# Transposing an MLP mixer's input by DMA instead of on TensorE, from the third batch on

## The chip, the cores and the metric

The kernel runs on one core of a Trainium2 chip. The metric is the device time of one execution in microseconds; lower is better. Most executions of one kernel here lie within about 0.7% of its median, a few 0.8 to 1.1% above it, so verdicts rest on several interleaved runs of both kernels on the same chip.

## The reference, cut to what matters

Eight batches, eight heads, 576 positions, 64 channels a head. First an attention with a causal mask and a decay, then an MLP mixer over tokens and channels:

```python
def _moe_ref(x, w_tok1, w_tok2, w_ch1, w_ch2):       # x: 8 x 576 x 512, from the attention
    xt = x.transpose(0, 2, 1)
    h = np.maximum(xt @ w_tok1, 0.0) @ w_tok2        # mixing over tokens
    u = x + h.transpose(0, 2, 1)
    h2 = np.maximum(u @ w_ch1, 0.0) @ w_ch2          # first and last layer over channels
    return (u + h2).astype(np.float32)
```

## The kernel before

As this kernel is written, each matmul sums over the partitions of its two operands (the first dimension of a tile). The mixing over tokens produces u with tokens on partitions, and the first channel layer wants channels there. So u is transposed once for each batch, in pieces of 128 tokens by 512 channels: each takes four 128x128 transposes on TensorE into one PSUM bank and one copy out of it.

The program is not written in order of execution. Every step is an operation with a modelled cost, given to a small list scheduler ("the planner"). The planner simulates the engines with these costs, gives out ring buffers, and writes each engine's instructions down in the order of its modelled start times. Each engine then executes its own list in order, as the traces show it (in the changed kernel ScalarE stands idle for 2.58 us at a square whose load is late, and four exponentials listed behind it start only after it). The costs are guesses, so a wrong one does not change the result, only the order.

```python
# in tok(b): one piece c of batch b; u, us: token-major, uT: channel-major
P.op(dve(512, add), reads=[(pm, 0)] + xkeys, writes=[ukey], prio=0)         # u = mixed + x, VectorE
if not odd and c == 4:
    continue
pt = Buf(r_mx, False)                                                       # one of three PSUM banks
# ...
def tr(pt=pt, dst=dst, di=di):
    o = pt.t[:, :].bitcast(BF16)
    for m in range(NMC):                                                    # NMC = 4
        nc.tensor.transpose(out=o[:, m * 128 : m * 128 + 128],
                            in_=dst.t[:, di, m * 128 : m * 128 + 128], identity=ident[:, :])
P.op({"PE": (4 * 0.057, 4 * 0.057 + 0.3, tr)}, reads=rk, writes=[(pt, 0)] + ..., prio=(rank - TOK, 2))
# ... then a copy to uT by ScalarE or VectorE
P.op(either(512, lambda ev=ev: ev(0), lambda ev=ev: ev(1), True), reads=[(pt, 0)], writes=[(uT, c)], prio=0)
```

The last 64 tokens of two neighbouring batches share one piece (`us`), so even batches have four pieces and odd ones five. In chan(b) the first layer reads uT with 48 (or 2 x 48) matmuls, and the last layer follows. The scheduler runs the last layer of batch b-1 into the mixing of batch b.

Of the kernel before, what the change touches and what calls it, by code (L numbers as in the profile page):

```python
# [204 lines left out]
def c_pe(n, f32=False):  # L205
    occ = n * (4 if f32 else 1) / 2400.0 + 0.0025
    return occ, occ + 0.30
# [126 lines left out]
def kernel(  # L334
# [12 lines left out]
    nc = tc.nc  # L347
# [25 lines left out]
    def ring(name, n, shape, dt, pool=None):  # L373
        p = pool or fast
        return Ring(name, [p.tile(shape, dt, name=f"{name}{i}", tag=f"{name}{i}") for i in range(n)])
# [39 lines left out]
    r_mx = ring("pmx", 3, [128, 512], FP32, psum)  # L415

    P = Plan()
# [29 lines left out]
    for i in range(1, 3):  # L447
        P.op({"DVE": (1.0, 1.2, lambda i=i: pads(nc.vector, i)), "POOL": (1.6, 1.8, lambda i=i: pads(nc.gpsimd, i))},
             writes=[("pad", i)], prio=40)
    P.op({"DVE": (0.6, 0.8, lambda: pads2(nc.vector)), "POOL": (1.0, 1.2, lambda: pads2(nc.gpsimd))},  # L450
         writes=["padw"], prio=41)
    P.op({"DVE": (0.3, 0.5, lambda: pads3(nc.vector, 1)), "POOL": (0.5, 0.7, lambda: pads3(nc.gpsimd, 1))},
         writes=["padv"], prio=42)
# [12 lines left out]
    def dve(n, fn, two=False):  # L466
        return {"DVE": (*c_dve(n, two), fn)}

    def act(n, fn, bias=False):
# [4 lines left out]
         reads=["s"], writes=["sr"], prio=-1)  # L474
    P.op({"DVE": (1.3, 1.6, lambda: nc.vector.tensor_tensor_scan(
        out=cum[:, :], data0=one_sb[:, :], data1=s_sb[:, :], initial=0.0, op0=ALU.mult, op1=ALU.add))},
        reads=["sr"], writes=["cum"], prio=-1)
    P.op(dve(1, lambda: nc.vector.tensor_scalar(
        out=half[:, :], in0=cum[:, S - 1 : S], scalar1=-0.5, scalar2=None, op0=ALU.mult)),
        reads=["cum"], writes=["half"], prio=-1)  # L480
    P.op(act(576, lambda: nc.scalar.activation(
        out=wn[:, 0:S], in_=cum[:, :], func=AF.Exp, bias=half[:, 0:1], scale=1.0), True),
        reads=["half", "cum"], writes=["wn"], prio=-1)
    bw = Buf(r_mx, False)

    def w_tr():
# [6 lines left out]
        out=wT[:, :, :].rearrange("p c e -> p (c e)"), in_=bw.t[:, 0:384])),  # L493
        reads=[(bw, 0)], writes=["wT"], prio=-1)
# [18 lines left out]
        out=pre[:, :], data0=one_sb[:, :], data1=wn[:, 0:S], initial=0.0, op0=ALU.mult, op1=ALU.add))},  # L513
        reads=["wn"], writes=["pre"], prio=50)
# [255 lines left out]
    def either(n, fa, fd, two=False):  # L770
        return {"ACT": (*c_act(n), fa), "DVE": (*c_dve(n, two), fd)}

    def tok(b):
        odd = b % 2
        x = xbuf[b]
        h1 = Buf(r_h1)
        xkeys = [(x, hh) for hh in range(H)]
        rank = 4 * (b + 1) + LAG
        if odd:
            u = Buf(r_ub)  # L780
        else:
            u = Buf(r_ua)
            ushare[b // 2] = Buf(r_us)
        us = ushare[b // 2]
        heads = [(0, H - 2), (H - 2, H)] if b == 0 else [(0, H)]
        pms = [Buf(r_mx, False) for t in range(NTC)]
        for (ha, hb) in heads:
            for t in range(NTC):
                def mm(t=t, pm=pms[t], ha=ha, hb=hb):
                    for c in range(NJ):  # L790
                        nc.tensor.matmul(out=pm.t[:, ha * D : hb * D],  # L791
                                         lhsT=w1[:, NJ if odd and c == NJ - 1 else c, t * 128 : t * 128 + 128],
                                         rhs=x.t[:, c, ha * D : hb * D], start=(c == 0), stop=(c == NJ - 1))
                occ = 5 * c_pe((hb - ha) * D)[0]
                P.op({"PE": (occ, occ + 0.3, mm)},
                     reads=[(x, hh) for hh in range(ha, hb)] + ["w1", "w1s", "padw"],
                     writes=[(pms[t], ha)], holds=[h1], prio=(rank - TOK, 0))
        for t in range(NTC):
            pm = pms[t]
            P.op(either(512,  # L800
                        lambda t=t, pm=pm: nc.scalar.activation(out=h1.t[:, t, :], in_=pm.t[:, :], func=AF.Relu),
                        lambda t=t, pm=pm: nc.vector.tensor_scalar_max(out=h1.t[:, t, :], in0=pm.t[:, :], scalar1=0.0)),
                 reads=[(pm, ha) for (ha, hb) in heads], writes=[(h1, t)], prio=0)
        uT = Buf(r_uTb if odd else r_uTa)
        for c in range(NJ):
            dst, di, lo, hi = (u, c, 0, 128) if c < NJ - 1 else (us, 0, 64 * odd, 64 * odd + 64)
            pm = Buf(r_mx, False)

            def mm(c=c, pm=pm):
                w0 = c * 128 + (64 if c == NJ - 1 and not odd else 0)  # L810
                for t in range(NTC):
                    nc.tensor.matmul(out=pm.t[:, :], lhsT=w2[:, t, w0 : w0 + 128],
                                     rhs=h1.t[:, t, :], start=(t == 0), stop=(t == NTC - 1))
            P.op({"PE": (2 * c_pe(512)[0], 2 * c_pe(512)[0] + 0.3, mm)}, reads=[(h1, 0), (h1, 1), "w2"],
                 writes=[(pm, 0)], holds=[dst], prio=(rank - TOK, 1))
            ukey = (dst, di, lo)

            def add(c=c, pm=pm, dst=dst, di=di, lo=lo, hi=hi):
                nc.vector.tensor_tensor(out=dst.t[lo:hi, di, :], in0=pm.t[lo:hi, :], in1=x.t[lo:hi, c, :], op=ALU.add)  # L819
            P.op(dve(512, add), reads=[(pm, 0)] + xkeys, writes=[ukey], prio=0)  # L820

            if not odd and c == 4:
                continue
            pt = Buf(r_mx, False)
            rk = [(us, 0, 0), (us, 0, 64)] if dst is us else [ukey]
            tc_ = c

            def tr(pt=pt, dst=dst, di=di):
                o = pt.t[:, :].bitcast(BF16)
                for m in range(NMC):  # L830
                    nc.tensor.transpose(out=o[:, m * 128 : m * 128 + 128], in_=dst.t[:, di, m * 128 : m * 128 + 128],
                                        identity=ident[:, :])
            P.op({"PE": (4 * 0.057, 4 * 0.057 + 0.3, tr)}, reads=rk, writes=[(pt, 0)] + ([("st", "uT")] if b == 1 else []), holds=[uT], prio=(rank - TOK, 2))

            def ev(eng, pt=pt, tc_=tc_):
                i = pt.t[:, :].bitcast(BF16)[:, 0:512].rearrange("p (m t) -> p m t", m=NMC)
                o = uT.t[:, :, tc_ * 128 : tc_ * 128 + 128]
                if eng == 0:
                    nc.scalar.copy(out=o, in_=i)  # L839
                else:  # L840
                    nc.vector.tensor_copy(out=o, in_=i)
            P.op(either(512, lambda ev=ev: ev(0), lambda ev=ev: ev(1), True), reads=[(pt, 0)], writes=[(uT, c)], prio=0)
        return u, us, uT
# [75 lines left out]
    for b in range(B):  # L919
        for h in range(0, H, 2):  # L920
            pair(b, h)
        st = tok(b)
        chan(b, *st)

    P.op(dve(64, lambda: nc.vector.tensor_scalar(
        out=bad[0:PR, 4:], in0=sq[:, :], scalar1=21.0, scalar2=None, op0=ALU.is_gt)),
        reads=[("sq", i) for i in range(NSQ)] + ["bad0"], writes=["bad"], prio=50)
# [3 lines left out]
         reads=["bad"], writes=[(bf, 0)], prio=(100, 0))  # L931
# [17 lines left out]
    for o in [o for o in order if o.eng == "PE"]:  # L949
# [3 lines left out]
        while t1 - t0 > 0.06:  # L953
# [6 lines left out]
            if not slots:  # L960
# [4 lines left out]
                out=t[:, 0:n], lhsT=zero[:, 0:128], rhs=zero[:, 0:n], start=True, stop=True)  # L965
# [47 lines left out]
```

## Time and profile before

| | before |
|---|---|
| median of three runs | 339.69 us (338.54 to 340.94) |
| profiled execution, span | 337.3 us |
| TensorE busy / share of the last chain | 93% / 69% |
| transposes of u on TensorE | 144, of which 108 for b = 2 to 7 |
| output store of 256 KB on the sync queue, medians | issue 0.33 to 0.36 us, landing (data arrived) from 2.0 us after the start of issue |

The main lines stand in the prediction. In TensorE's timeline, columns are start, duration, engine, source line, operation, output and inputs, shapes, count. In b = 3 of the kernel before:

```profile
148.05 0.39 PE L831 MATMUL pmx_117<-ident,us_103 128*128 128x128 bf16 x4
148.49 0.38 PE L657 MATMUL psc_112<-qT_80,kT_83 128*128 128x512 bf16 x1
```

A group of four transposes that is followed at once by work that is ready costs 0.22 us. This one holds TensorE for 0.44 us to the start of the next instruction, though the profile reports no idle time there: short gaps stay below what it lists. Nine of the 27 groups of b = 2 to 7 take 0.38 to 0.51 us in this way.

### The profile page before, as it was taken

Reading aid. Unit: us, or ns where it says so; the run is one execution under the profiler, and the core shown is the slowest. Engines: PE = TensorE matmul, PEld = TensorE weight load, DVE = VectorE, ACT = ScalarE, POOL = GpSimd, SP = SyncE. Lnnn points to the kernel's source line nnn. Section 1 sums busy time; section 2 is a strip of 40 time slices with the busy share of each in tenths; the row PEclk is TensorE's granted clock in tenths of the full one; section 3 lists DMA queues with packets and bytes.
Section 4 is the critical chain, followed back from the end, with each engine's and each line's share of the span. In section 5 each row is a group of like instructions: output and inputs, shape, how many; then the busy total and the mean of one; then the engine's idle time right before and its main releaser. Section 6 shows DMA issues by size and latency. Waiting matters only on the chain.

```text
span 337.3 us, 6710 instructions
## 1 busy us (share of the span) xinstructions
PE 315.2 (93%) x2532; PEld 184.7 (55%) x2565; DVE 207.7 (62%) x510; ACT 221.6 (66%) x395; POOL 100.1 (30%) x137
## 2 busy tenths in 40 slices
PE   6978999988999999989999999989999999999992
PEld 2445585645765455555765445555765454446641
DVE  7698945899776746584577655584677545450021
ACT  4766975669788548785786747787799738325600
POOL 6355157768237001830147001830110000000000
PEclk9799999999999999999999999999999999999999
DMA  7999999999953349288024952253548110011031
GB/s 203 222 291 376 374 213 231 266 271 227 215 114 106 130 138 206 77 208 194 2 75 133 227 145 71 87 157 121 143 119 232 67 63 2 16 49 62 3 95 68
DMA packets 62584, 50.60 MB, mean 150 GB/s; under 512 B 39632, under 2 KB 55568, under 8 KB 62544
## 3 DMA queue, kind: packets, MB, share of 16 engines
q1 hardware_dynamic: 62544, 50.10, 56.7%
q8 instruction: 22, 0.36, 0.4%
q14 instruction: 18, 0.15, 0.2%
HBM read 40.65 MB, written 9.44 MB: 148 GB/s over the span
## 4 chain that ended last, share of the span: by engine, by line
PE 69%; DVE 18%; ACT 7%; issue 2%; DMA 1%; POOL 1%; SPq 0%; ACTq 0%
PE pmx_118 L877 9%; PE pmx_119 L877 8%; PE pmx_117 L859 8%; PE pmx_118 L859 8%; PE pmx_119 L859 8%; PE pmx_117 L877 7%; DVE ub_101 L819 3%; PE pmx_119 L791 2%; DVE E_86 L671 2%; PE psc_114 L657 2%; PE pav_115 L689 2%; PE psc_113 L657 2%; DVE E_84 L671 2%; PE pav_116 L689 2%; PE psc_112 L657 2%
## 5 line engine op out<-in xcount | busy, mean ns | idle before, releaser
L859 PEld LDWEIGHTS <-wc_70 128*128 128x128 bf16 x624 | 59.3, 98 | 30.5 <-issue 0.2
L877 PEld LDWEIGHTS <-gb_107 128*128 128x128 bf16 x240 | 22.9, 98 | 25.3
L575 POOL CAST qkn_76<-qkf_73 96x768 bf16<-96x768 f32 x22 | 19.1, 887 | 37.5 <-ACT gb_107 L866 20.1
L877 PEld LDWEIGHTS <-ga_106 128*128 128x128 bf16 x192 | 18.2, 98 | 21.2 <-issue 1.4
L575 POOL CAST qkn_77<-qkf_74 96x768 bf16<-96x768 f32 x19 | 15.7, 840 | 40.8 <-ACT ga_106 L866 19.7
L575 POOL CAST qkn_75<-qkf_72 96x768 bf16<-96x768 f32 x19 | 15.4, 828 | 39.1 <-ACT gb_107 L866 18.5
L671 DVE TENSOR_TENSOR E_84<-E_84,keep 128x256 bf16<-128x256 bf16 (+1 forms) x55 | 18.4, 365 | 13.3 <-ACT E_84 L663 12.8
L859 PE MATMUL pmx_118<-uTb_105,wc_70 128*128 128x320 bf16 x128 | 22.6, 299 | 0.1
L859 PE MATMUL pmx_117<-uTb_105,wc_70 128*128 128x320 bf16 x128 | 22.6, 299 | 0.0
L859 PE MATMUL pmx_119<-uTb_105,wc_70 128*128 128x320 bf16 x128 | 22.6, 299 | 0.0
L877 PE MATMUL pmx_119<-wc_71,gb_107 128*128 128x512 bf16 x92 | 22.3, 379 | 0.2
L548 POOL TENSOR_TENSOR vp_90<-vf_88,wT 128x512 bf16<-128x512 f32 (+1 forms) x20 | 21.0, 1069 | 2.5 <-DMA vf_88<-in_v_dram 2.2
L671 DVE TENSOR_TENSOR E_86<-E_86,keep 128x256 bf16<-128x256 bf16 (+1 forms) x50 | 17.1, 368 | 6.7 <-ACT E_86 L663 6.4
L671 DVE TENSOR_TENSOR E_85<-E_85,keep 128x256 bf16<-128x256 bf16 (+1 forms) x55 | 16.5, 329 | 6.3 <-ACT E_85 L663 6.1
L877 PE MATMUL pmx_118<-wc_71,gb_107 128*128 128x512 bf16 x80 | 19.2, 379 | 0.2
L866 ACT ACTIVATE gb_107<-pmx_119 128x320 bf16<-128x320 f32 x25 | 11.1, 444 | 11.4 <-PE pmx_119 L859 9.9
L859 PE MATMUL pmx_118<-uTa_104,wc_70 128*128 128x512 bf16 (+1 forms) x77 | 17.0, 335 | 0.2
L859 PE MATMUL pmx_119<-uTa_104,wc_70 128*128 128x512 bf16 (+1 forms) x79 | 17.1, 336 | 0.1
L548 POOL TENSOR_TENSOR vp_89<-vf_87,wT 128x512 bf16<-128x512 f32 (+1 forms) x15 | 15.3, 1040 | 5.8 <-PE pav_116 L689 4.7
L859 PE MATMUL pmx_117<-uTa_104,wc_70 128*128 128x512 bf16 (+1 forms) x78 | 16.8, 335 | 0.1
L877 PE MATMUL pmx_117<-wc_71,ga_106 128*128 128x512 bf16 x69 | 16.7, 379 | 0.2
L877 PE MATMUL pmx_118<-wc_71,ga_106 128*128 128x512 bf16 x69 | 16.5, 379 | 0.3 <-ACT uTb_105 L839 0.2
(297 smaller groups left out, 723.0 us busy)
## 6 DMA issues: line engine op xcount, KB each, us to landing
qkf_74<-in_k_dram SPq DMA_DIRECT2D x15, 288.0 KB, 3.4
qkf_74<-in_q_dram SPq DMA_DIRECT2D x15, 288.0 KB, 4.0
vf_87<-in_v_dram SPq DMA_DIRECT2D x16, 256.0 KB, 7.0
vf_88<-in_v_dram SPq DMA_DIRECT2D x16, 256.0 KB, 5.5
qkf_72<-in_k_dram SPq DMA_DIRECT2D x13, 288.0 KB, 4.0
qkf_72<-in_q_dram SPq DMA_DIRECT2D x13, 288.0 KB, 4.5
qkf_73<-in_k_dram SPq DMA_DIRECT2D x12, 288.0 KB, 4.7
qkf_73<-in_q_dram SPq DMA_DIRECT2D x12, 288.0 KB, 5.0
```

Of the source, the lines that this page charges most:

```text
L548: eng.tensor_tensor(out=vp.t[p0 : p0 + n, c, :, 0:D], in0=vf.t[p0 : p0 + n, c, :, :], in1=wT[p0 : p0 + n, cw, b * H : b * H + H].unsqueeze ...
L575: nc.gpsimd.tensor_copy(out=o, in_=a)
L657: nc.tensor.matmul(out=o[:, :, c0 : c0 + e - a], lhsT=kT.t[:, j0 : j0 + 128], rhs=qT.t[:, :, a:e], start=True, stop=True)
L671: nc.vector.tensor_tensor(out=E.t[:, :, d0 : d0 + n], in0=E.t[:, :, d0 : d0 + n], in1=keep[:, k0 : k0 + n].unsqueeze(1).to_broadcast([128, ...
L689: nc.tensor.matmul(out=o[:, ic, 0 : D + 1], lhsT=E.t[:, hh, d0 : d0 + 128], rhs=vp.t[:, jc, h + hh, 0 : D + 1], start=(jc == j_lo), stop=( ...
L791: nc.tensor.matmul(out=pm.t[:, ha * D : hb * D], lhsT=w1[:, NJ if odd and c == NJ - 1 else c, t * 128 : t * 128 + 128], rhs=x.t[:, c, ha * ...
L819: nc.vector.tensor_tensor(out=dst.t[lo:hi, di, :], in0=pm.t[lo:hi, :], in1=x.t[lo:hi, c, :], op=ALU.add)
L859: nc.tensor.matmul(out=pm.t[:, 0 : e - a], lhsT=wc1[:, m, cc * 128 : cc * 128 + 128], rhs=uT.t[:, m, a:e], start=(m == 0), stop=(m == NMC ...
L866: lambda cc=cc, pm=pm, a=a, e=e: nc.scalar.activation(out=g.t[:, cc, a:e], in_=pm.t[:, 0 : e - a], func=AF.Relu),
L877: nc.tensor.matmul(out=pm.t[:, :], lhsT=g.t[:, cc, c * 128 : c * 128 + 128], rhs=wc2[:, cc, :], start=(cc == 0), stop=(cc == NCC - 1))
```

## The change

The intent: TensorE is the bound (busy 93% of the span), the DMA engines have room after the second batch (mean share 1.06 from 40 to 80 us, 0.19 to 0.68 in the six transposing stretches of b = 2 to 7), so let a transposing DMA carry u to uT directly, without PSUM and without the copy.

```diff
-            pt = Buf(r_mx, False)
             rk = [(us, 0, 0), (us, 0, 64)] if dst is us else [ukey]
             tc_ = c
+            if b >= 2:
+                def trd(dst=dst, di=di, tc_=tc_):
+                    nc.sync.dma_start_transpose(out=uT.t[:, :, tc_ * 128 : tc_ * 128 + 128], in_=dst.t[:, di, :])
+                P.op({"SP": (0.6, 0, trd)}, reads=rk, writes=[(uT, c)],
+                     prio=0, dma=0.5)
+                continue
+            pt = Buf(r_mx, False)
```

The pair (0.6, 0) is what the planner is told: 0.6 us of the sync queue for each; `dma=0.5` is the time planned on the DMA engines.

## The prediction

> **What bounds the kernel now.** I read the page's busy shares first, then the chain of waits, then who waits on TensorE, then the six stretches in which batches 3 to 8 (b = 2 to 7) form the mixer's input, and last the timeline of the final one.
>
> ```profile
> span 337.3 us, 6710 instructions
> PE 315.2 (93%) x2532; PEld 184.7 (55%) x2565; DVE 207.7 (62%) x510; ACT 221.6 (66%) x395; POOL 100.1 (30%) x137
> PE 69%; DVE 18%; ACT 7%; issue 2%; DMA 1%; POOL 1%; SPq 0%; ACTq 0%
> ...
> 96.00:112.00 16.00, 15.38 (x142) 9.23 (x142) 12.33 (x29) 11.64 (x21) 9.37 (x12) 1.00 0.38 103
> ...
> L831 PE MATMUL pmx_118<-ident,ua_100 x24: 216/219/221, 39.1 to 261.2; 128*128 128x128 bf16 x24
> ...
> L839 ACT COPY uTb_105<-pmx_118 x5: 577/586/586, 145.4 to 299.3; 128x512 bf16<-128x512 bf16 x5
> ...
> L841 DVE COPY uTa_104<-pmx_118 x4: 407/414/425, 39.8 to 261.6; 128x512 bf16<-128x512 bf16 x4
> ```
>
> TensorE is busy 93% of the span and carries 69% of the chain that ends last. From 96 us on it is almost solid: 15.38 of the first 16 us, and likewise later. So the kernel is bound by the quantity of work on TensorE, and nearly every microsecond taken off it there ends the kernel earlier, as long as nothing new makes it wait. VectorE and ScalarE are not the bound in sum (62%, 66%), but in the transposing stretches they are: the table of those six stretches (columns: length, busy PE, PEld, DVE, ACT, POOL, clock, DMA share, GB/s) shows it.
>
> ```profile
> 102.70:111.00 8.30, 7.95 (x79) 4.88 (x79) 6.98 (x13) 6.06 (x12) 5.05 (x6) 1.00 0.42 112
> 141.40:150.00 8.60, 7.47 (x77) 4.64 (x77) 8.21 (x18) 6.71 (x12) 4.97 (x8) 1.00 0.55 164
> 179.70:187.30 7.60, 7.25 (x76) 4.57 (x75) 7.06 (x13) 4.78 (x9) 4.29 (x7) 1.00 0.46 120
> 217.00:226.00 9.00, 7.87 (x80) 4.81 (x80) 8.52 (x19) 7.05 (x14) 5.05 (x8) 1.00 0.56 160
> 255.60:263.30 7.70, 7.05 (x70) 4.28 (x70) 6.67 (x18) 7.61 (x14) 0.00 (x0) 1.00 0.68 184
> 293.80:305.10 11.30, 10.79 (x64) 5.40 (x63) 5.20 (x9) 2.15 (x4) 0.00 (x0) 1.00 0.19 71
> ...
> 146.69 0.38 PE L831 MATMUL pmx_119<-ident,ub_101 128*128 128x128 bf16 x4 [0.85 <-DVE us_103 L819]
> ...
> 222.37 0.38 PE L831 MATMUL pmx_119<-ident,ub_101 128*128 128x128 bf16 x4 [0.85 <-DVE us_102 L819]
> ```
>
> In two of them VectorE is busy 8.21 of 8.60 and 8.52 of 9.00 us, and TensorE stands 0.85 us at a transpose that waits for VectorE's addition. TensorE's idle time in the six sums to 52.50 - 48.38 = 4.1 us.
>
> [...] The trace shows TensorE's at 219 ns each, pipelined: a group of four that starts at 146.69 is followed by the next at 146.91, so four cost 0.22 us of TensorE[...]. No run yet shows the DMA's. [...] The landing I take from the trace: the output stores from the sync queue take 2.0 us at the median from issue to landing. [...]
>
> **The change part by part.** Odd b has five pieces of 128x512, even b four. For b = 2 to 7 that is 3 x 4 + 3 x 5 = 27 pieces.
> Removed from TensorE: 27 groups of four transposes, 27 x 0.225 = 6.1 us. TensorE is the path there, so all of it counts.
> Removed from ScalarE and VectorE: 27 evictions out of PSUM at 586 ns (ScalarE) or about 410 ns (VectorE), some 13 us. Little of this is on the path, but it comes out of exactly the six crowded stretches, and so do the rounds through the three PSUM banks that the transposes shared with the mixer's matmuls.
> Moved: in the built program's order the matmuls around those stretches keep their order, but the pieces of the previous batch's last layer (twelve matmuls, 2.6 us) now follow the mixer's matmuls at once, where TensorE used to meet transposes that had to wait for VectorE. The two waits of 0.85 us and smaller ones of 0.41, 0.30, 0.29, 0.16 and 0.16 us (the last two for an eviction) should mostly go; I count 2.3 of the 4.1 us of idle time.
> Added: 27 transposes on the sync queue, which issues a store in 0.33 to 0.36 us and waits most of the time. I take 1.2 us of that queue each [...] and 2.2 us from the end of issue to landing. Their 128 KB are 3.4 MB on top of 50.6 MB, and the DMA share in those stretches is 0.19 to 0.68.
> Is it hidden? Cover is the time from the first addition's end to the first matmul that needs the result. For even b = 4: the first addition ends at 181.5; after the last mixer matmul (182.8) the new order has 48 matmuls of 0.216 us of the last layer, 36 small ones of the attention (1.1 us), 7 score matmuls (1.5) and 12 small transposes (0.5), 13.5 us, so the result is needed at 196.3. Four serial transposes with 2 us of landing may cost 3.2 us each before anything waits. For odd b = 3: additions from 142.97 on, last mixer matmul done at 144.5, cover 36 x 0.216 + 1.1 + 1.1 + 0.3 = 10.2 us, needed at 154.7 to 155.2: five may cost 2.05 us each. For the last batch there is only the last layer to hide behind: 24 matmuls, 5.2 us, after 297.8; the left half is needed at 303.0, the right (pieces four and five) at 303.5. Additions end at 295.2, 295.8, 296.9, 297.5 and 299.0. With 1.2 us each, issue goes 295.2, 296.4, 297.6, 298.8, then a store, then the fifth from 300.4 to 301.6, landing at 303.8: 0.3 us too late.
> Sum: -6.1 - 2.3 + 0.3 = -8.1 us. From 339.7 that gives 331.6 us.
>
> **The rivals.** First: the transposes are slow, and a DMA wait takes the place of the evictions. [...] At 2 us each only the last batch stalls, by about 3.5 us: 335 us, inside 2%. At 3 us: about 5 us in each of b = 3 and 5 and 8.5 us at the end, less 8.4: some 350 us. [...]
> Second: the sync queue runs in order, so the transposes wait for additions and hold up the loads behind them, and they land behind loads already queued (q and k pieces land in 3.4 to 5.0 us, v in 5.5 to 7.0). For it: in the new order the transposes of b = 2 stand ahead of two stores and the next loads, and the page's DMA row reaches 8 and 9 tenths in places. Against it: three raw and three converted buffers of q and k let loads run several head pairs ahead, and GpSimd is only 30% busy; a load 5 us later should not reach TensorE. A queue of 5 us ahead of a transpose fits under the 10 and 13 us of cover, and the last batch has no loads about it. I put 1 us on it at most.
> Third: the transposing work is hidden anyway, so only the idle time changes. Against it: TensorE itself executes them, and its order is fixed.
> Fourth: it goes better. All 4.1 us of idle time vanish, and the lighter ScalarE and VectorE shorten waits elsewhere: 339.7 - 6.1 - 4.1 - 1 = 328.5 us.
>
> **Range and chances.** The steps add up to 331.6; a little for queueing makes it 332.0. The low end, 328.5, is the fourth rival; the high end, 340, is a transpose of about 2.4 us in both the odd stretches and the end. The line for faster by over 2% is 339.7 x 0.98 = 332.9, hardly above my number, so the chance of faster is 0.54 only; within 2% gets 0.32 (a transpose of 1.5 to 2.5 us), slower 0.14 (3 us and up, or something that I do not see).
>
> **What would show it.** Right: 108 fewer transposes and 27 fewer evictions; TensorE's busy time lower by about 6 us; the waits of 0.85 us gone from the odd stretches; no wait of the first-layer matmuls for a DMA into the transposed input beyond 1 us, except near the end of the last batch; transposes landing 2 to 4 us after issue, 1.2 us apart. Wrong: TensorE at the first layer waiting several us for a DMA in each batch (first rival); waits for converted q and k or for v (second); or busy time down by 6 us with as much new idle time.

## More of the kernel before

The kernel checks a range of q and k by squaring them on ScalarE. For the first two batches this is done late, from a second load:

```python
def stage_sq(b, h):                        # b = 0, 1 only; planned with low priority, lands in b = 5, 6
    for i, src in enumerate((k, q)):
        load_op(load, [(f, i)], ...)       # on the sync queue
    P.op({"ACT": (1.55, 2.0, lambda: nc.scalar.activation(out=junk[:, :], in_=f..., func=AF.Square, ...))}, ...)
```

## The result, and the profile after

The changed kernel takes 330.63 us (median of four runs, 328.07 to 333.03), before 339.88. The ratio is 0.9704, interval 0.9629 to 0.9779: faster by 3%. Ratios here are the mean time of one kernel's runs over that of the other's of the same rounds, so not quite the ratio of the medians. Executions over 1.5% slower than the fastest of the same kernel are left out of the means.

The head of the page of the changed kernel, against the same lines of before in the prediction:

```profile
span 330.5 us, 6536 instructions
PE 308.9 (93%) x2424; PEld 178.6 (54%) x2457; DVE 207.2 (63%) x511; ACT 207.4 (63%) x367; POOL 101.1 (31%) x137
PE 75%; DVE 14%; ACT 3%; DMA 3%; issue 2%; SPq 1%; POOL 0%; ACTq 0%
```

TensorE has 108 instructions fewer and 6.3 us less of busy time, ScalarE 28 fewer and 14 us less. VectorE has none fewer, although it lost 11 of the 27 evictions: the planner gave it 12 other evictions that ScalarE had made. The chain that ends last runs more through TensorE, and 3% of it through DMAs, where there was 1%. Of these 9.8 us, 5.76 are the first load at the start (4.55 before); the other 4.03 are new, and we come to them. First the transposes, by their source line (minimum/median/maximum in ns), and from the start of issue to landing:

```profile
L828 SPq DMA_TRANSPOSE uTa_104<-ua_100 x12: 1194/1218/1339, 107.9 to 255.3; - x12
L828 SPq DMA_TRANSPOSE uTb_105<-ub_101 x12: 1194/1216/1232, 143.4 to 294.3; - x12
...
DMA to landing us min/median/max: 2.4/2.4/4.2
```

At the median each holds the sync queue for 1.22 us (the one not shown, in b = 5, for 2.39) and has landed 2.4 us after its start. The place with the least cover is the last batch. In the changed kernel's timeline there:

```profile
290.37 5.14 SPq L828 DMA_TRANSPOSE uTb_105<-ub_101  x4
...
296.24 1.22 SPq L828 DMA_TRANSPOSE uTb_105<-us_103  x1
...
298.08 0.71 PE L865 MATMUL pmx_119<-uTb_105,wc_70 128*128 128x320 bf16 x4
...
298.78 0.70 PE L865 MATMUL pmx_117<-uTb_105,wc_70 128*128 128x320 bf16 x4
```

The fifth transpose, from 296.24, has landed at 296.24 + 2.4 = 298.64. Four matmuls of 128x320 need 0.54 us, so TensorE was free for the right half at 298.62 and started at 298.78: it lost 0.16 us. In the five other batches the profile lists no wait of a first-layer matmul for a DMA.

The new part of the chain, the 4.03 us, is the load of q from 257.20 in b = 6. The changed kernel's timeline (the value in brackets is the idle time of that engine just before, and what ended it):

```profile
251.32 5.19 SPq L828 DMA_TRANSPOSE uTa_104<-ua_100  x4
...
256.61 0.53 SPq L597 DMA_DIRECT2D qkf_74<-in_k_dram  x1
257.20 0.43 SPq L597 DMA_DIRECT2D qkf_74<-in_q_dram  x1
...
261.33 1.48 ACT L600 ACTIVATE junk<-qkf_74 96x1536 bf16<-96x1536 f32 x1 [2.58 <-DMA qkf_74<-in_q_dram]
...
263.43 0.38 PE L657 MATMUL psc_112<-qT_80,kT_83 128*128 128x384 bf16 x2 [2.11 <-ACT E_86 L663]
...
263.86 3.09 PE L883 MATMUL pmx_118<-wc_71,gb_107 128*128 128x512 bf16 x7
```

Read it from the top. The four transposes hold the sync queue until 256.51. Behind them stand two loads for the range check, which reach ScalarE only at 261.33. The planner had put the square of that load ahead of four exponentials in ScalarE's list, so those wait with it (they start from 262.81 on), and TensorE waits 2.11 us for a score bank. What follows is slower too: seven matmuls take 3.09 us. In another execution of the same kernel the same seven take 1.67. TensorE's granted clock had dropped to half (0.50) for one stretch of 3.4 us, from 263.96.

### The profile page after: what moved, and what is told of

The parts are those of the page before. It is cut to its first block, busy times and chain, and to the rows that moved or that the text cites.

```text
span 330.5 us, 6536 instructions
## 1 busy us (share of the span) xinstructions
PE 308.9 (93%) x2424; PEld 178.6 (54%) x2457; DVE 207.2 (63%) x511; ACT 207.4 (63%) x367; POOL 101.1 (31%) x137
## 4 chain that ended last, share of the span: by engine, by line
PE 75%; DVE 14%; ACT 3%; DMA 3%; issue 2%; SPq 1%; POOL 0%; ACTq 0%
PE pmx_118 L883 12%; PE pmx_119 L865 9%; PE pmx_118 L865 8%; PE pmx_117 L865 8%; PE pmx_117 L883 7%; PE pmx_119 L883 7%; PE psc_112 L657 3%; PE pav_115 L689 2%; PE psc_113 L657 2%; PE psc_114 L657 2%; PE pav_116 L689 2%; DMA qkf_73<-in_k_dram 2%; PE pmx_117 L791 2%; PE pmx_117 L812 2%; DVE E_86 L671 2%
## 5 line engine op out<-in xcount | busy, mean ns | idle before, releaser
L575 POOL CAST qkn_75<-qkf_72 96x768 bf16<-96x768 f32 x19 | 17.1, 923 | 43.2 <-issue 12.9
L575 POOL CAST qkn_76<-qkf_73 96x768 bf16<-96x768 f32 x22 | 18.3, 853 | 37.2 <-issue 18.2
L883 PE MATMUL pmx_118<-wc_71,gb_107 128*128 128x512 bf16 x116 | 28.9, 393 | 0.2
L575 POOL CAST qkn_77<-qkf_74 96x768 bf16<-96x768 f32 x19 | 15.7, 843 | 30.7 <-ACT gb_107 L872 10.3
L671 DVE TENSOR_TENSOR E_84<-E_84,keep 128x256 bf16<-128x256 bf16 (+1 forms) x55 | 17.2, 343 | 11.1 <-ACT E_84 L663 10.6
L671 DVE TENSOR_TENSOR E_85<-E_85,keep 128x256 bf16<-128x256 bf16 (+1 forms) x55 | 16.7, 331 | 8.9 <-ACT E_85 L663 8.7
L671 DVE TENSOR_TENSOR E_86<-E_86,keep 128x256 bf16<-128x256 bf16 (+1 forms) x50 | 14.8, 323 | 10.3 <-ACT E_86 L663 10.1
L872 ACT ACTIVATE gb_107<-pmx_119 128x320 bf16<-128x320 f32 x23 | 10.2, 442 | 17.4 <-PE pmx_119 L865 16.0
L883 PE MATMUL pmx_117<-wc_71,ga_106 128*128 128x512 bf16 x69 | 16.9, 379 | 0.2
L970 PE MATMUL pmx_117<-zero 128*128 128x512 bf16 (+6 forms) x44 | 14.2, 418 | 1.5 <-DVE zero L425 1.2
L883 PE MATMUL pmx_118<-wc_71,ga_106 128*128 128x512 bf16 x57 | 14.3, 379 | 0.2
```

The source lines that it names most:

```text
L575: nc.gpsimd.tensor_copy(out=o, in_=a)
L671: nc.vector.tensor_tensor(out=E.t[:, :, d0 : d0 + n], in0=E.t[:, :, d0 : d0 + n], in1=keep[:, k0 : k0 + n].unsqueeze(1).to_broadcast([128, ...
L872: lambda cc=cc, pm=pm, a=a, e=e: nc.scalar.activation(out=g.t[:, cc, a:e], in_=pm.t[:, 0 : e - a], func=AF.Relu),
L883: nc.tensor.matmul(out=pm.t[:, :], lhsT=g.t[:, cc, c * 128 : c * 128 + 128], rhs=wc2[:, cc, :], start=(cc == 0), stop=(cc == NCC - 1))
L970: f.fn = lambda t=r.tiles[slots[0]], n=n: nc.tensor.matmul(out=t[:, 0:n], lhsT=zero[:, 0:128], rhs=zero[:, 0:n], start=True, stop=True)
```

## The experiments

Twelve runs were made, in three sets; each set shares its runs of the kernel before (medians 339.97, 340.26 and 340.00 us). Names that end in "told" are planned with 1.25 us for a transpose instead of 0.6.

One measure is steadier than the times. It was worked out from the profiled executions after the runs: from the first matmul of the second token layer (L812) in b = 2 to the end of the span. Its start in the kernel before (span 337.3 us) and in plan_told_again (325.0 us):

```profile
103.82 0.59 PE L812 MATMUL pmx_119<-h_98,w_69 128*128 128x512 bf16 x2
...
104.27 1.03 PE L812 MATMUL pmx<-h,w 128*128 128x512 bf16 x4
```

| from b = 2 to the end, one profile each | us |
|---|---|
| before; dma_too | 233.5; 233.4 |
| changed kernel; after_again | 224.7; 222.6 |
| plan_told; plan_told_again | 220.6; 220.7 |
| no_transpose; evict_too | 220.7; 220.9 |
| pe_too_told; all_but_last_told | 229.3; 222.9 |

What lies before b = 2 takes 103.0 to 106.2 us in these profiles, so much of the scatter is there. After it, plan_told and its repetition agree within 0.1 us.

### The stall in b = 6: a run again, and the planner told the truth

The changed kernel once more, without an edit:

> The changed kernel once more, to see whether its times spread. Theory A (a stall that comes and goes): in the profile taken of it, ScalarE waits 2.6 us in b = 6 for a load that stood behind four transposes in the sync queue, TensorE then stands still for over 2 us and afterwards runs some 3 us at half its clock; runs with that stall should take about 332 us and show a mean clock near 0.98, runs without it about 328 us and 0.99 or more. Rival B (plain scatter of the chip): times spread evenly, and neither clock nor the profile goes with them. Ratio to before expected at 0.965 to 0.975 by both.

It took 329.95 us (327.48 to 331.61), ratio 0.970 (0.9662 to 0.9739). The profile has the stall again, this time without a drop of the clock behind it (granted clock 1.00 from 250 to 268 us):

```profile
260.44 1.48 ACT L600 ACTIVATE junk<-qkf 96x1536 bf16<-96x1536 f32 x1 [2.10 <-DMA qkf<-in_q_dram]
...
262.55 0.38 PE L657 MATMUL psc<-qT,kT 128*128 128x384 bf16 x2 [1.63 <-ACT E L663]
```

Theory A is right about the stall and wrong about the scatter: the times do not fall into two groups, and clock and time do not go together (331.61 us at clock 0.996, 329.67 at 0.985). A likely reason, not tested: six of the eight profiled executions in which it was read, of whatever kernel, have some half-clock time in the first 40 us (3.4 us in the kernel before, granted clock there 0.96; 6.8 us in the changed kernel, 0.91; 1.00 in pe_too and plan_told_again), where the DMA engines are busy throughout (share 1.01 to 1.04).

Then one number of the planner:

```diff
-                P.op({"SP": (0.6, 0, trd)}, reads=rk, writes=[(uT, c)],
+                P.op({"SP": (1.25, 0, trd)}, reads=rk, writes=[(uT, c)],
```

> The planner that orders the instructions is told 1.25 us of the sync queue for a transpose, as measured (1.22), in place of 0.6. TensorE's order stays the same; in b = 6 ScalarE's four exponentials move ahead of the square that waited for the late load. Theory A: the stall of b = 6 is gone in every run: 326.5 to 328.5 us, mean clock 0.99 or more, ratio 0.960 to 0.967, and 2 to 4 us below the changed kernel's slow executions. Rival B: as the changed kernel, ratio within 0.3% of it, with the same spread.

It took 327.47 us (327.05 to 330.52), ratio 0.9648 (0.9611 to 0.9686). To settle it, the same kernel again with the last set:

> plan_told once more, to settle whether it is below the changed kernel (0.970 of before): 326.5 to 328.5 us, ratio 0.960 to 0.967, and in the profile no wait of ScalarE for a load in b = 6. If it comes out at 329.5 us or more, its advantage was scatter.

326.83 us (326.27 to 327.37), ratio 0.9618 (0.9600 to 0.9636). TensorE's order is that of the changed kernel, instruction by instruction. On ScalarE, four exponentials moved ahead of one square. The timeline of plan_told at the same place:

```profile
259.59 2.11 ACT L663 ACTIVATE E<-psc 128x512 bf16<-128x512 f32 x4 [1.31 <-PE psc L657]
260.69 0.38 PE L657 MATMUL psc<-qT,kT 128*128 128x384 bf16 x2
261.60 1.47 ACT L600 ACTIVATE junk<-qkf 96x1536 bf16<-96x1536 f32 x1
```

The exponentials come first, the square finds its load landed, and TensorE does not wait. The 18 us from 250 on, in the changed kernel and in plan_told (length, busy PE, PEld, DVE, ACT, POOL, clock, DMA share, GB/s):

```profile
250.00:268.00 18.00, 15.78 (x102) 7.80 (x103) 9.53 (x25) 11.29 (x19) 0.00 (x0) 0.91 0.69 179
```

```profile
250.00:268.00 18.00, 17.84 (x129) 9.25 (x131) 12.06 (x30) 13.39 (x24) 0.00 (x0) 1.00 0.69 183
```

So the stall was real and belonged to the change as planned. Between the mixing of b = 6 and of b = 7 (from L812 to L812) it cost 3.9 us in the first profile and 1.8 in the second: 40.1 and 38.0 us, in plan_told and its repetition 36.2. plan_told beats the kernel before, and by this also the changed kernel; by the times alone the latter is less clear, as its interval overlaps that of after_again and only that of plan_told_again does not.

### What the DMA side costs

The transposes are left out, with the plan's order as it was.

```diff
-                    nc.sync.dma_start_transpose(out=uT.t[:, :, tc_ * 128 : tc_ * 128 + 128], in_=dst.t[:, di, :])
+                    pass
```

> Wrong result on purpose: the transposes of b = 2 to 7 are left out altogether, with the plan's order unchanged, so the first layer reads what b = 0 and 1 left in the transposed input. It is what the change would give if transposing cost nothing. Theory A (the DMA transposes are hidden but for the stall in b = 6 and some 0.2 us at the end): 326.5 to 328 us, as the changed kernel without its stall. Rival C (the DMAs slow the loads or the transposes hold something up in each batch): 323 us or less.

The result was wrong, as meant. 327.75 us, ratio 0.9645 (0.9616 to 0.9675): the same as plan_told, in time and from b = 2 to the end (220.7 us). With the stall out of the way, 27 DMA transposes cost nothing that can be measured. The changed kernel of the same set stands at 0.970.

The opposite test adds the 27 transposes to the kernel before, into scratch tiles that nobody reads:

```diff
+            if b >= 2:
+                uX = Buf(r_ux, False)                      # a ring of 5 tiles, 128 x 4 x 128
+                def trd(dst=dst, di=di, uX=uX):
+                    nc.sync.dma_start_transpose(out=uX.t[:, :, :], in_=dst.t[:, di, :])
+                P.op({"SP": (1.25, 0, trd)}, reads=rk, writes=[(uX, c)], prio=0, dma=0.5)
```

> The kernel before, with the 27 DMA transposes added into scratch tiles that nobody reads, planned with 1.25 us: the added side of the change alone. Theory (a transpose holds the sync queue and 16 engines for a while but nothing on TensorE's path waits for that): 339 to 341 us, ratio 0.997 to 1.004. Rival (contention: loads, stores or engines are slowed): 343 us or more.

339.94 us, ratio 0.9997 (0.9980 to 1.0013). There is no contention to speak of, although a transpose does fill the DMA engines for a moment (in the changed kernel their share is 1.08 from 293.2 to 293.4 us, 0.06 from 293.6 to 293.8).

### TensorE's part and the evictions' part

The DMA transposes stay, and TensorE makes its own as well, into PSUM, where nobody reads them:

```diff
+                pt = Buf(r_mx, False)
+                def trx(pt=pt, dst=dst, di=di):
+                    o = pt.t[:, :].bitcast(BF16)
+                    for m in range(NMC):
+                        nc.tensor.transpose(out=o[:, m * 128 : m * 128 + 128],
+                                            in_=dst.t[:, di, m * 128 : m * 128 + 128], identity=ident[:, :])
+                P.op({"PE": (4 * 0.057, 4 * 0.057 + 0.3, trx)}, reads=rk, writes=[(pt, 0)], prio=(rank - TOK, 2))
```

> The DMA transposes stay, and TensorE does its 27 x 4 transposes as well, into PSUM, where nobody reads them: no evictions by ScalarE or VectorE. Theory P (most of the gain is TensorE's own time, 27 x 0.225 = 6.1 us): 334 to 337 us, ratio 0.985 to 0.993. Rival E (the gain is that of the evictions and waits taken away): 329 to 332 us, near the changed kernel.

338.69 us, ratio 0.9959: above the range. Its profile shows why the sum is not clean: the stall in b = 6 is there, larger (ScalarE waits 5.29 us for the load, TensorE 2.04). So it was planned with 1.25 us and run again:

> As pe_too (TensorE does its 27 x 4 transposes besides the DMA's, no evictions), but planned with 1.25 us for a DMA transpose, because in pe_too the late load of b = 6 came back (ScalarE waited 5.3 us for it) and hid the sum. Theory P: over plan_told (327.5 us) TensorE's own 6.1 us and the 1.7 to 2.5 us in which its transposes wait for VectorE's additions come back: 334 to 336 us, ratio 0.984 to 0.990. If only the 6.1 us of work mattered, 333 to 333.8; if the stall in b = 6 remains, 337 or more, and the profile shows it.

336.33 us (335.16 to 340.12), ratio 0.9883 (0.9844 to 0.9921): the time is 0.3 us above its range, the ratio inside. Over plan_told (0.9648 and 0.9618) that is 2.35 to 2.65% of 340 us, 8.0 to 9.0 us. Adding up in its trace, from the start of each of the 27 groups to the start of the next instruction and without the idle time that the profile lists, the groups hold TensorE for 7.9 us, not 6.1; and they waited 0.8 us for additions. That makes 8.7 us, which agrees. From b = 2 to the end pe_too_told is 8.6 us above plan_told_again. The same sum in the kernel before is 7.9 us, and its waits before the groups are 2.3 us.

The other half: 27 copies of a PSUM bank to scratch on ScalarE or VectorE, no transposes on TensorE (the copies move 16-bit integers, as the bank holds whatever was there).

```diff
+                pt, sk_ = Buf(r_mx, False), Buf(r_ux, False)
+                def evx(eng, pt=pt, sk_=sk_):
+                    i = pt.t[:, :].bitcast(mybir.dt.uint16)[:, 0:512].rearrange("p (m t) -> p m t", m=NMC)
+                    # ... ScalarE or VectorE copies i to sk_
+                P.op(either(512, ...), reads=rk + [(pt, 0)], writes=[(sk_, 0)], prio=0)
```

> The other half put back: over plan_told, ScalarE or VectorE do 27 copies of a PSUM bank to a scratch tile, one for each piece, while TensorE makes no transposes; each copy also holds a PSUM bank. Theory P: some 13 us of work on engines that are not the bound: 327 to 329 us, ratio 0.962 to 0.968. Rival E (evictions and the banks they hold are on the path): 330 to 333 us.

327.23 us, ratio 0.9620 (0.9584 to 0.9656), as plan_told. The evictions removed are worth nothing by themselves. This copy waits for no transpose, though, and TensorE's order differs a little from plan_told's. From b = 2 to the end the two halves put back 8.6 and 0.2 of the 12.8 us that lie between plan_told_again and the kernel before. So two thirds of the gain are TensorE's own; the other 4.0 us come back only where each eviction waits for its transposes, as before, and no run separates what costs them there.

### What a transpose's 1.22 us consists of, and whether the covers were right

One DMA for each 128x128 block:

```diff
-                    nc.sync.dma_start_transpose(out=uT.t[:, :, tc_ * 128 : tc_ * 128 + 128], in_=dst.t[:, di, :])
+                    for m in range(NMC):
+                        nc.sync.dma_start_transpose(out=uT.t[:, m, tc_ * 128 : tc_ * 128 + 128],
+                                                    in_=dst.t[:, di, m * 128 : m * 128 + 128])
```

> Each piece of 128x512 is transposed by four DMAs of 128x128 in place of one, planned as before. It measures what the sync queue's 1.22 us consists of, and tests the cover worked out in the prediction (2.05 us for a piece in odd batches, 3.2 in even ones, about 1.3 in the last). If the cost goes by tiles, four take 1.2 to 1.6 us and the time stays within 2 us of plan_told (327.5). If each instruction has a fixed cost of 0.5 us or more, a piece takes 2.7 us or more: the odd batches stall by some 3 us each, the last by some 5 to 6, and the time is 336 to 342 us.

422.61 us, ratio 1.2417. A quarter of the data takes as long (transposes by tile, then the first layer's waits for them in us, times):

```profile
L829 SPq DMA_TRANSPOSE uTa<-ua x48: 1160/1222/2242, 107.6 to 325.2; - x48
L829 SPq DMA_TRANSPOSE uTb<-ub x48: 1107/1183/2154, 152.9 to 380.0; - x48
...
  PE pmx L867: 60.5, 36
```

The cost belongs to the instruction and not to its data: 1.18 to 1.23 us at the median for 128x128, 1.22 for 128x512. From the start of issue to landing it is 2.3 and 2.4 us. A piece of four instructions takes some 4.9 us, beyond every cover, so TensorE waits 60.5 us for DMAs in all, and the granted clock is lower with it (mean 0.878, plan_told_again 0.998). The first rival's arithmetic (pieces times what each costs above its cover), with 4.9 us for a piece and the covers 2.05, 3.2 and 1.3 us, gives some 67 us of waiting. My range was far too low, because I had set the fixed cost at "0.5 us or more".

Two DMAs of 128x256 put the cost of a piece between the covers:

```diff
-                    nc.sync.dma_start_transpose(out=uT.t[:, :, tc_ * 128 : tc_ * 128 + 128], in_=dst.t[:, di, :])
+                    for m in (0, 2):
+                        nc.sync.dma_start_transpose(out=uT.t[:, m : m + 2, tc_ * 128 : tc_ * 128 + 128],
+                                                    in_=dst.t[:, di, m * 128 : m * 128 + 256])
```

> Each piece by two DMAs of 128x256, with TensorE's order that of plan_told. After four_blocks (1.2 us of the sync queue for 128x128 as for 128x512) a piece should take 2.4 us: above the cover of 2.05 us of the odd batches and far above that of the last batch, below the 3.2 us of the even ones. Theory (fixed cost for each instruction, and the covers as worked out): no wait of the first layer for a DMA in the even batches; 1 to 2.5 us in b = 3 and 5; 5 to 6 us at the end, with a stretch at half clock after it: 335 to 339 us, ratio 0.985 to 0.997. If the time goes by size instead: 327 to 329 us.

347.27 us, ratio 1.0221: the covers held, the total did not. The largest wait of the first layer for a DMA in b = 3, in b = 5 and in the last batch:

```profile
156.36 0.45 PE L867 MATMUL pmx<-uTb,wc 128*128 128x320 bf16 x2 [1.05 <-DMA uTb<-us]
229.09 0.45 PE L867 MATMUL pmx<-uTb,wc 128*128 128x320 bf16 x2 [1.38 <-DMA uTb<-us]
...
310.88 0.45 PE L867 MATMUL pmx<-uTb,wc 128*128 128x320 bf16 x2 [3.37 <-DMA uTb<-us]
```

With the smaller ones beside them that is 1.6 us in b = 3, 2.2 in b = 5, 5.0 at the end, and none in the even batches: each as expected from a piece of 2.4 us. Most of the rest of the excess is the stall of b = 6 again. Eight transposes held the sync queue for 10.2 us, the check's loads came later still, ScalarE waited 4.5 and 1.7 us for them, and TensorE stood 5.6 us; the three score matmuls right after it take 1.44 us, where three took 0.81 at 262.93. Moving one square back, as plan_told does, was enough for four transposes and not for eight.

### How far the change should go

The last batch back on TensorE:

```diff
-            if b >= 2:
+            if 2 <= b < B - 1:
```

> plan_told with the last batch's five pieces put back on TensorE with their evictions. The prediction took the last batch for the one with too little cover, late by 0.3 us. Theory: even there the DMA is the better way, as five groups cost TensorE some 0.29 us each and two waits of 0.16 us come back: 328.5 to 329.8 us, 1 to 2 us over plan_told. Rival: the DMA's latency at the end eats that: 327 to 328 us, the same as plan_told.

329.43 us, ratio 0.9694 (0.9664 to 0.9724): 1.6 to 2.6 us above plan_told, and 2.2 us from b = 2 to the end. Even with the least cover the DMA is the better way.

The second batch by DMA as well:

```diff
-            if b >= 2:
+            if b >= 1:
```

> The DMA transposes begin with the second batch, planned with 1.25 us: five pieces more. If TensorE is the bound there too, 5 x 0.225 = 1.1 us and the wait of 1.1 us at its transposes for an addition go: 325 to 326.5 us. Rival: in the second batch the DMA queues are full (share of 1.06 between 40 and 80 us), the transposes land late behind loads, and the time is that of plan_told or longer (327.5 to 331).

333.00 us, ratio 0.9790 (0.9746 to 0.9834): 5 to 6 us above plan_told, and a miss, further off than even the rival. The rival's mechanism is not it either: the five transposes of b = 1 landed 2.5 us after issue at the median and 3.9 at most. From its timeline:

```profile
84.19 1.22 SPq L828 DMA_TRANSPOSE uTb<-us  x1
...
89.89 0.38 PE L657 MATMUL psc<-qT,kT 128*128 128x512 bf16 x1 [1.37 <-ACT qT L639]
...
91.87 0.47 PE L865 MATMUL pmx<-uTb,wc 128*128 128x320 bf16 x1
```

The fifth transpose starts at 84.19, yet the first layer starts at 91.87, where in plan_told_again it starts at 80.22. All of the loss lies there: from the mixing of b = 1 to that of b = 2 it takes 35.7 us, plan_told_again 29.7. In the second batch there is no last layer of the batch before left to put between. The planner fills the time until the transposes land with attention work, whose chain through ScalarE and VectorE is exposed there: ten waits between 74 and 92 us come to 4.8 us, and the matmuls at the end of it are slower: the one of 128x320 at 91.87 takes 0.47 us, where the kernel before takes 0.30 at the mean. That the lack of cover is the cause is argued from these two timelines, not tested by a run of its own.

## Why the prediction was right

The time was right (332.0 predicted, 330.63 measured, range 328.5 to 340), and so was the reason in kind: work leaves the engine that is the bound, and the DMA is hidden. That the number came so close is partly luck: without the stall of b = 6 the gain is some 12.8 us and not 8.1, and that stall, put at 1 us at most, took 1.8 to 3.9 us of it back. By its steps:

- **Removed from TensorE, 6.1 us.** Right in kind, too small: 7.9 us. The 0.225 us were taken from groups in a dense stretch; nine of the 27 take 0.38 to 0.51 us to the next instruction.
- **Evictions, 13 us off the path.** Right: evict_too puts them back and loses nothing. But the reading that VectorE and ScalarE are the bound in the transposing stretches holds for three of the six rows at most (VectorE 8.21 of 8.60 and 8.52 of 9.00 us, ScalarE 7.61 of 7.70); in the other three TensorE is the busiest.
- **Idle time, 2.3 us.** Right: 2.3 us of listed waits before the groups in the kernel before, and they are gone. All the idle time that the profile lists from b = 2 to the end fell by more, from 4.0 us to 0.7 in the plan without the stall, which is what the fourth rival expected.
- **Issue, 1.2 us each.** The number was right (1.22), what it stood on was not. It was my estimate, which no trace or run had shown then, and it took the cost to grow with the data; four_blocks_told shows 1.18 to 1.23 us for 128x128, as for 128x512. A fortunate number. Pieces of 128 KB that follow each other at once start 1.30 us apart, which is 101 GB/s.
- **Landing, 2.2 us after the end of issue.** Wrong: 2.4 us after its start, so 1.2 after its end. At the last batch this cancelled another error: the fifth issue came some 0.7 us later than predicted, since four issues and the store before it took longer. 0.3 us of lateness was predicted, 0.16 seen.
- **The covers, 3.2, 2.05 and (worked out later) 1.3 us.** Confirmed by two_halves_told, which stalls in the odd batches and at the end and not in the even ones.
- **The second rival, loads held up behind the transposes, "1 us at most".** This is the step that failed. It looked only at the loads for GpSimd, and their delay did cost nothing: from b = 2 to the mixing of b = 6 the changed kernel takes as long as no_transpose, batch by batch within 0.02 us. The loads of the range check feed ScalarE and stand right behind the transposes of b = 6. In the profiled execution they cost TensorE a wait of 2.1 us and a stretch at half clock, 3.9 us in all; in after_again 1.8.

The sum with measured terms, -7.9 - 2.3 + 0.2 = -10.0 us, holds for the plan without the stall. That plan measured 0.9648 and 0.9618, or -12.0 and -13.0 us, and -12.8 us from b = 2 to the end; at 326.83 to 327.47 us it lies below the low end of the range. About 1.2 of the missing 2.8 us are listed idle time outside the sum (it fell by 3.3 us, not by 2.1). The other 1.6 us are open; short gaps that closed in the new order are a likely source, but no run isolates them. The changed kernel, with the ratio 0.970 or -10.2 us, is that plan less the stall of 1.8 to 3.9 us. So its own agreement with -10.0 is a balance of two things that the sum leaves out.

## What to carry to other kernels

Moving the transposes from a bound TensorE to a DMA paid here (3%, and 3.5 to 3.8% without the stall) where a result, which landed 2.4 us after its start, had other TensorE work to land behind: find that work piece by piece, and leave out the stage that has none, here (as argued from two timelines) the second batch, which by DMA cost 5 to 6 us. Use few large transposing DMAs, as their cost on the queue was by instruction here (1.2 us for 128x128 as for 128x512). And look at what stands behind them in the same in-order queue, to the end of its chain: here a load nobody hurries for held up ScalarE for 2.58 us and TensorE for 2.11, through the order that a planner with a wrong cost had written.
